# The order of the first MLP block: three columns of h and one of o before any small products, then one run of small products between half columns

## The chip, the cores and the metric

The kernel runs on one core of one Trainium2 chip. The metric is the device time of one launch in microseconds (us); the time of a kernel is the median of its runs. TensorE is called PE below, VectorE DVE, ScalarE ACT, GpSimd POOL, SyncE SP.

## What is computed

Three stages follow each other on float32 data (batch 4, 8 heads, 768 steps, head size 48):

```python
# delta-rule attention: a 48x48 state per batch and head
k_n = k / (np.linalg.norm(k, axis=-1, keepdims=True) + 1e-06)
for t in range(S):
    y[:, :, t] = np.einsum('bhd,bhde->bhe', q[:, :, t], state)
    v_old = np.einsum('bhde,bhd->bhe', state, kt)
    state = state + bt[:, :, :, None] * np.einsum('bhd,bhe->bhde', kt, vt - v_old)
# first MLP, 384 -> 2048 -> 384 on 3072 tokens
h = x @ w_in
g = np.maximum(h, 0.0) + alpha * np.minimum(h, 0.0)
x = g @ w_out
# second MLP, 384 -> 1536 -> 384
g = x @ w_gate
out = (g * (1.0 / (1.0 + np.exp(-g))) * (x @ w_val)) @ w_out
```

## The kernel before

The attention is cut into 24 chunks `c` of 32 steps, and four chunks make a window `w`. Chunk `c` needs, in this order: `do_KS` (product `pk`), `do_QS` (`py`), `do_U` (`pu`, then `U`), `do_S` (the state, products `pst`, then the additions into `St`), `do_Y` (`py`) and `do_XT` (`px`, which gives `xh` and `xl`, the input of the first MLP). All of these products are small: they use 32 or 48 rows of the PE array, and a call of one of these functions is 32 float32 products in the program, which PE runs as 64. `pre_T` (`pt`, four wide transposes) and `pre_G` (`pg`) prepare `q` and `k` of a window, `mask_m` masks one result of `pre_G` on POOL. `lanes` inverts the small triangular matrices of a window on DVE and POOL, step by step; the first one here is that of window 1.

The first MLP takes two chunks of tokens as a block `n` of 256 columns and runs over 16 columns `j` of 128 features. `H1(n, j)` is nine wide products into `h`, ended by one ACT and one DVE instruction that make `pn`. `H1_parts` splits `pn` into a high part (ACT) and a low part (POOL, line 702), both in `gh`. `O1(n, j)` is nine wide products with `gh` into `o`: six with the high part and then three with the low part. `h` and `o` of one `j` are called half columns below. They take their weights from `w1[j]`, which `all_w1` makes from the raw weights pair by pair: DMA, ACT (line 592), three steps on DVE (597, 599, 603), ACT (887) and two subtractions on POOL (875).

The order of all this is written out by hand. Every step is put into a list with a time `u` by `at(u, fn, ...)`, the list is sorted by `u`, and the steps are issued in that order; each engine then runs its instructions strictly in it. The unit of `u` is one column of the first MLP: `H1(n, j)` stands at `16 * n + j`, `O1(n, j)` at 2.5 after it (3.6 for the first column of a later block). The prelude before the list brings chunks 0 and 1 to their end, so that block 0 can start; in the 16 columns of block 0 stand the work on chunks 2 and 3 (which block 1 needs), the rest of `q` of window 1, the remaining conversions of weights, three per column, and from 10.9 on `lanes` of window 1.

Of the kernel before, what the change touches and what calls it, by code (L numbers as in the profile page):

```python
# [24 lines left out]
def kernel(  # L25
# [68 lines left out]
    nat = [ap.tile([128, H, 2, 64], F32, name=f"nat{z}") for z in range(2)]  # L94
# [43 lines left out]
    def half_rows(b):  # L138
        return slice(64 * (b // 2), 64 * (b // 2) + D)
# [19 lines left out]
    def kq_of(c):  # L159
        return kqt[c // 2][:, c % 2]  # L160

    def bank(early, name):
        pool, tag = (ps_h1, "h1") if early else (ps_a, "a")
        return pool.tile([128, 512], F32, name=name, tag=tag)
# [32 lines left out]
    def pre_G(c, parts=(0, 1), early=False, raw=False):  # L197
        w, ci = divmod(c, 4)
        kq = kq_of(c)
        if ci == 0 and 0 in parts:  # L200
            GL[w] = ap.tile([128, 32, C], F32, name="GL", tag="lane" if w > 1 else "TT", bufs=2)
        ps = bank(early, "pg")
        n0, n1 = parts[0], parts[-1] + 1
        for h in range(H):
            for b in BS:
                r = half_rows(b)
                nc.tensor.matmul(  # L207
                    ps[32 * b:32 * b + 32, h * 64 + n0 * C:h * 64 + n1 * C],
                    kq[r, b % 2, h, 0, :],
                    kq[r, b % 2, h, n0:n1, :],  # L210
                    start=True,
                    stop=True,
                    skip_group_check=True,
                )
        gv = ps.rearrange("p (h n i) -> p h n i", h=H, n=2)
        if 0 in parts:
            nc.scalar.activation(out=GL[w][:, ci * 8:ci * 8 + 8, :], in_=gv[:, :, 0, :], func=AF.Copy)
        if 1 in parts:
            mt = ap.tile([128, H, C], F32, name="mt", tag="mt", bufs=6)
            if raw:  # L220
                nc.scalar.activation(out=mt, in_=gv[:, :, 1, :], func=AF.Copy)
            else:
                nc.vector.tensor_tensor(mt, gv[:, :, 1, :], mask.unsqueeze(1).to_broadcast([128, H, C]), ALU.mult)
            m_t[c] = mt
# [88 lines left out]
    def lanes(w, cut):  # L313

        t = Lanes(w)

        def eliminate(i, eng, c0, c1, tmp):

            n, m = C - 1 - i, min(i + 1, c1) - c0
            if m <= 0:  # L320
                return
            w = tmp[:, 0:n * m].rearrange("p (a b) -> p a b", a=n)
            eng.tensor_tensor(  # L323
                w,
                t.L[:, i + 1:C, i:i + 1].to_broadcast([128, n, m]),
                t.X[:, i:i + 1, c0:c0 + m].to_broadcast([128, n, m]),
                ALU.mult,
            )
            yield
            Xv = t.X[:, i + 1:C, c0:c0 + m]  # L330
            eng.tensor_tensor(Xv, Xv, w, ALU.subtract)  # L331

        t.turn(0)
        yield
        t.turn(1)
        GL.pop(w)
        yield
        t.new_X()
        t.norm()
        t.length(0)  # L340
        yield
        for i in range(2):
            r = slice(i * HC, i * HC + HC)
            nc.vector.tensor_tensor(
                t.L[:, :, r], t.L[:, :, r], t.a.unsqueeze(2).to_broadcast([128, C, HC]), ALU.mult
            )
            yield
        size = [max((C - 1 - i) * (min(i + 1, c1) - c0) for i in range(C)) for c0, c1 in ((0, cut), (cut, C))]
        tv = t.new("tmp", "tmp", [128, size[0]])
        tg = t.new("tmg", "tmg", [128, size[1]])  # L350
        for i in range(C - 1):
            todo = [eliminate(i, nc.vector, 0, cut, tv)]
            if i + cut < C - 1:
                todo.append(eliminate(i + cut, nc.gpsimd, cut, C, tg))
            for z in range(2):
                for g in todo:
                    next(g, None)
                t.length(2 * i + z + 1)
            if i == HC:
                TT_t[w] = t.new("TT", "TT", [128, 32, C], 2)  # L360
                t.turn_X(0)
            yield
        t.turn_X(1)
        yield
# [490 lines left out]
    inv0 = []  # L855

    def at(u, fn, *args):
        events.append((u, len(events), fn, args))
# [41 lines left out]
    def go(g, n=1):  # L900
        for _ in range(n):
            next(g, None)
# [101 lines left out]
        return inv  # L1004

    def base(c):
        return {2: 2.9, 3: 7.7, 4: 22.6, 5: 27.2}.get(c, 8 * (c - 2))

    CONV_DONE, CONV_END = 8 + sum(CONVS), 11.0
    CONV_N = 3 * J1 + 1 - CONV_DONE  # L1010
# [2 lines left out]

    for w in range(1, NWIN):
        P = base(4 * w) - 32
        if w == 1:
            for z in range(2):
                at(1.4 + 1.2 * z, lambda: go(inv0[0]))
            for z in range(4):
                at(1.8 + 1.05 * z, pre_T, 1, "q", z // 2, z % 2, nat)  # L1020
            for z in range(4):
                at((5.7, 7.0, 8.8, 10.4)[z], lambda z=z: pre_G(4 + z, raw=True))
                at(13.0 + 2 * z, mask_m, 4 + z)
            for z in range(2):
                at((4.3, 6.4)[z], lambda z=z: pre_G(2 + z, (1,), raw=True))
                at((4.9, 7.5)[z], mask_m, 2 + z)
            l0, l1, n = 10.9, 22.6, LANES
        else:
            if w < TURN:
                at(P - 5, load_nat, w, "k", nat)  # L1030
                for z in range(4):
                    at(P + 1.2 + z, pre_T, w, "k", z // 2, z % 2, nat)
                at(P + 4.5, load_nat, w, "q", nat)
                for z in range(4):
                    at(P + 7.2 + z, pre_T, w, "q", z // 2, z % 2, nat)
            else:
                for z in range(4):
                    at(P - 13 + 1.5 * z, load_split, w, "k", z, nat)
                    at(P - 6.5 + 0.8 * z, turn_T, w, "k", z, nat)
                    at(P - 5.6 + 1.2 * z, load_split, w, "q", z, nat)  # L1040
                    at(P + 3.0 + z, turn_T, w, "q", z, nat)
            at(P - 1, load_beta, w)
            for z in range(4):
                at(P + 11.2 + z, pre_G, 4 * w + z)
            l0, l1, n = P + 15, P + 31.5, LANES
        box = {}

        def step(w=w, box=box):
            if "g" not in box:
                box["g"] = lanes(w, 10)  # L1050
            next(box["g"], None)

        for z in range(n):
            at(l0 + (l1 - l0) * z / n, step)

    at(0.5, do_S, 1)
    at(0.6, load_k2, 2)
    for c in range(2, NCH):
        u = base(c)
        f = {2: 0.8, 3: 0.8, 4: 0.6, 5: 0.6}.get(c, 1.0)  # L1060
        if c > 2:
            at(u - 7, load_v, c)
            at(u - 1.3, load_k2, c)
        at(u - 1.5, scale_v, c)
        at(u + 0.3, do_KS, c)
        at(u + 0.35, do_QS, c)
        at(u + 0.3 + 2 * f, do_U, c)
        at(u + 0.3 + 4 * f, do_S, c)
        at(u + 0.3 + 5 * f, do_Y, c)
        at(u + 0.3 + (7 if c < 4 else 6) * f, do_XT, c)  # L1070
    for n in range(NB1):
        for j in range(J1):
            at(16 * n + j, H1, n, j)
# [33 lines left out]
    for n in range(NB2):  # L1107
        u = E1 + LA + 1 + J2 * n
# [43 lines left out]
```

## Time and profile before

| | us |
|---|---|
| median of 3 runs (1093.03 to 1093.74) | 1093.32 |
| the profiled execution | 1094.43 |
| its span, first to last instruction | 1092.5 |
| PE busy | 1055.2 (97%) |
| DVE busy | 603.6 (55%) |
| ACT busy | 389.9 (36%) |
| POOL busy | 359.5 (33%) |

The profiled execution lies 1.1 us above the median, and 1.9 us of it lie outside its span. In a timeline a row gives the start, the time to the end of its last product, the engine, the line, and in brackets how long the engine stood idle before it and for whom; "issue" is a wait for nothing that the profile shows. The granted clock of PE is 1.0 at 2.4 GHz and 0.5 at 1.2 GHz.

### The profile page before, as it was taken

Reading aid. Unit: us, or ns where it says so; the run is one execution under the profiler, and the core shown is the slowest. Engines: PE = TensorE matmul, PEld = TensorE weight load, DVE = VectorE, ACT = ScalarE, POOL = GpSimd, SP = SyncE. Lnnn points to the kernel's source line nnn. Section 1 sums busy time; section 2 is a strip of 40 time slices with the busy share of each in tenths; the row PEclk is TensorE's granted clock in tenths of the full one; section 3 lists DMA queues with packets and bytes.
Section 4 is the critical chain, followed back from the end, with each engine's and each line's share of the span. In section 5 each row is a group of like instructions: output and inputs, shape, how many; then the busy total and the mean of one; then the engine's idle time right before and its main releaser. Section 6 shows DMA issues by size and latency. Waiting matters only on the chain.

```text
span 1092.5 us, 35673 instructions
## 1 busy us (share of the span) xinstructions
PE 1055.2 (97%) x15649; PEld 969.6 (89%) x15649; DVE 603.6 (55%) x1204; ACT 389.9 (36%) x841; POOL 359.5 (33%) x531
## 2 busy tenths in 40 slices
PE   6689899999999999999999999999999999999998
PEld 5588788999999999999999998888888888888887
DVE  5778865975895697489453453433333333333332
ACT  3556343343434334433444653222222222222211
POOL 3478852832563383366333541101001001010000
PEclk9669999999999999999999999999999999999999
DMA  9663042353344236330441541010010010100001
GB/s 196 184 192 105 10 103 53 62 122 95 70 69 134 66 62 139 90 82 11 118 130 56 159 135 54 1 58 1 1 58 1 18 42 1 58 1 1 29 1 29
DMA packets 165979, 76.34 MB, mean 70 GB/s; under 512 B 129824, under 2 KB 160576, under 8 KB 165824
## 3 DMA queue, kind: packets, MB, share of 16 engines
q1 hardware_dynamic: 160256, 66.28, 24.5%
q10 hardware_dynamic: 5184, 7.37, 2.2%
q8 instruction: 122, 2.00, 0.8%
q0 software_dynamic: 384, 0.41, 0.2%
q14 instruction: 33, 0.27, 0.1%
HBM read 57.52 MB, written 16.52 MB: 68 GB/s over the span
## 4 chain that ended last, share of the span: by engine, by line
PE 89%; POOL 4%; issue 2%; DVE 2%; DMA 1%; ACT 1%; SPq 0%; ACTq 0%; POOLq 0%; DVEq 0%
PE gv L772 27%; PE o L713 18%; PE h L682 18%; PE o L802 14%; PE pst L527 2%; PE pg L207 2%; PE pu L506 2%; PE py L548 2%; PE pk L462 2%; PE py L462 1%; POOL w L875 1%; DMA nat<-in_k_dram 1%; POOL gh L702 1%; POOL X L331 1%; POOL tmg L323 1%
## 5 line engine op out<-in xcount | busy, mean ns | idle before, releaser
L772 PE MATMUL gv<-x2s,w 128*128 128x512 f32 x1296 | 307.6, 391 | 0.0
L772 PEld LDWEIGHTS gv<-x2s,w 128*128 128x128 f32 x1296 | 242.5, 188 | 47.8
L713 PE MATMUL o<-gh,w 128*128 128x256 f32 x1728 | 246.2, 288 | 3.9 <-POOL gh L702 3.9
L682 PE MATMUL h<-xh,w 128*128 128x256 f32 x1152 | 241.2, 286 | 3.0 <-DVE pn L693 1.6
L702 POOL TENSOR_TENSOR gh<-pn,gh 128x256 fp32r<-128x256 f32 x192 | 155.3, 809 | 248.5 <-ACT gh L701 217.3
L713 PEld LDWEIGHTS o<-gh,w 128*128 128x128 f32 x1728 | 217.3, 189 | 11.5 <-POOL gh L702 5.1
L682 PEld LDWEIGHTS h<-xh,w 128*128 128x128 f32 x1152 | 192.2, 191 | 5.8 <-DVE pn L693 2.6
L693 DVE SCALAR_TENSOR_TENSOR pn<-pn,slope,h 128x256 f32<-128x256 f32 x192 | 91.3, 476 | 135.9 <-ACT pn L692 135.9
L682 PE MATMUL h<-xl,w 128*128 128x256 f32 x576 | 163.2, 283 | 0.1
L802 PE MATMUL o<-w,us 128*128 128x384 f32 x864 | 162.5, 337 | 0.0
L802 PEld LDWEIGHTS o<-w,us 128*128 128x128 f32 x864 | 151.9, 188 | 7.1 <-DVE os L815 1.4
L692 ACT ACTIVATE pn<-h,slope 128x256 f32<-128x256 f32 x192 | 90.4, 471 | 137.7 <-PE h L682 134.5
L784 DVE TENSOR_TENSOR sg<-sg,gv 128x512 f32<-128x512 f32 x72 | 49.5, 687 | 151.8 <-ACT sg L782 151.7
L701 ACT ACTIVATE gh<-pn 128x256 fp32r<-128x256 f32 x192 | 80.0, 417 | 145.0 <-DVE pn L693 143.2
L682 PEld LDWEIGHTS h<-xl,w 128*128 128x128 f32 x576 | 109.8, 191 | 0.6 <-DVE xl L574 0.6
L757 POOL TENSOR_TENSOR x2s<-x2r,x2s 128x512 fp32r<-128x512 f32 x15 | 19.3, 1320 | 266.6 <-ACT x2s L755 266.6
L789 ACT ACTIVATE us<-u 128x512 fp32r<-128x512 f32 x72 | 45.5, 632 | 171.2 <-DVE u L785 171.2
L782 ACT ACTIVATE sg<-gv 128x512 f32<-128x512 f32 x72 | 43.0, 597 | 159.3 <-PE gv L772 159.3
L790 DVE TENSOR_TENSOR us<-u,us 128x512 fp32r<-128x512 f32 x72 | 49.9, 693 | 54.8 <-ACT us L789 54.8
L785 DVE TENSOR_TENSOR u<-sg,gv 128x512 f32<-128x512 f32 x72 | 49.5, 688 | 49.3 <-PE gv L772 48.8
L331 DVE TENSOR_TENSOR X<-X,tmp 128x31 f32<-128x31 f32 (+29 forms) x155 | 65.0, 419 | 4.8
L323 DVE TENSOR_TENSOR tmp<-L,X 128x31 f32<-128x31 f32 (+29 forms) x155 | 59.5, 384 | 1.8
(120 smaller groups left out, 975.9 us busy)
## 6 DMA issues: line engine op xcount, KB each, us to landing
w<-in_moe_w_out_dram SPq DMA_DIRECT2D x19, 384.0 KB
wf<-w2d SPq DMA_DIRECT2D x36, 192.0 KB
k<-in_k_dram SPq DMA_DIRECT2D x96, 48.0 KB
x2d<-xs SPq DMA_DIRECT2D x12, 384.0 KB
w<-in_moe_w_gate_dram SPq DMA_DIRECT2D x12, 384.0 KB
w<-in_moe_w_val_dram SPq DMA_DIRECT2D x12, 384.0 KB
x2r<-x2d SPq DMA_DIRECT2D x24, 192.0 KB
v<-in_v_dram SPq DMA_DIRECT2D x88, 48.0 KB
```

Of the source, the lines that this page charges most:

```text
L323: eng.tensor_tensor(w, t.L[:, i + 1:C, i:i + 1].to_broadcast([128, n, m]), t.X[:, i:i + 1, c0:c0 + m].to_broadcast([128, n, m]), ALU.mult,)
L331: eng.tensor_tensor(Xv, Xv, w, ALU.subtract)
L682: nc.tensor.matmul(ps[:, 0:N1], w[:, a, kk * 128:kk * 128 + 128], x[b][:, kk, :], start=(i == 0), stop=(i == 3 * NK - 1),)
L692: nc.scalar.activation(out=g, in_=hv, func=AF.Relu, scale=slope[:, 0, j:j + 1])
L693: nc.vector.scalar_tensor_tensor(out=g, in0=g, scalar=slope[:, 1, j:j + 1], in1=hv, op0=ALU.mult, op1=ALU.add)
L701: nc.scalar.activation(out=gh[:, 0], in_=g, func=AF.Copy)
L702: nc.gpsimd.tensor_tensor(gh[:, 1], g, gh[:, 0], ALU.subtract)
L713: nc.tensor.matmul(o[:, dm // 2, (dm % 2) * N1:(dm % 2) * N1 + N1], w[:, a, dm * 128:dm * 128 + 128], g[:, b], start=(j == 0 and i == 0 an ...
L772: nc.tensor.matmul(p[:, 0:N2], w2[j, z][:, a, kk * 128:kk * 128 + 128], x[:, b, kk], start=(i == 0), stop=(i == 3 * NK - 1),)
L784: nc.vector.tensor_tensor(sg, sg, ps[0], ALU.mult)
L790: nc.vector.tensor_tensor(us[:, 1], u, us[:, 0], ALU.subtract)
L802: nc.tensor.matmul(o2_t[n][t][:, 0:DM], us[:, a, t * 128:t * 128 + 128], w[:, b, :], start=(j == 0 and i == 0), stop=(j == J2 - 1 and i == 2),
```

## The change

Only times in the list change, all of them for the work beside block 0. The first state update (`do_S(1)`) and the load that follows it move from 0.5 to 2.6, so that `H1` of columns 0 to 2 and `O1` of column 0 stand ahead of them. The steps of chunks 2 and 3, the four `pre_T`, the two remaining steps of the prelude's inversion (`go(inv0[0])`), the `pre_G` of window 1 and of chunks 2 and 3, and two of the masks get times that leave one of them, or one with a `pre_T` of four transposes, between any two half columns.

```diff
-        return {2: 2.9, 3: 7.7, 4: 22.6, 5: 27.2}.get(c, 8 * (c - 2))
+        return {2: 3.4, 3: 7.8, 4: 22.6, 5: 27.2}.get(c, 8 * (c - 2))
...
             for z in range(2):
-                at(1.4 + 1.2 * z, lambda: go(inv0[0]))
+                at(3.1 + z, lambda: go(inv0[0]))
             for z in range(4):
-                at(1.8 + 1.05 * z, pre_T, 1, "q", z // 2, z % 2, nat)
+                at((3.7, 4.7, 5.15, 5.65)[z], pre_T, 1, "q", z // 2, z % 2, nat)
             for z in range(4):
-                at((5.7, 7.0, 8.8, 10.4)[z], lambda z=z: pre_G(4 + z, raw=True))
+                at(6.6 + z, lambda z=z: pre_G(4 + z, raw=True))
                 at(13.0 + 2 * z, mask_m, 4 + z)
             for z in range(2):
-                at((4.3, 6.4)[z], lambda z=z: pre_G(2 + z, (1,), raw=True))
-                at((4.9, 7.5)[z], mask_m, 2 + z)
+                at((5.6, 10.6)[z], lambda z=z: pre_G(2 + z, (1,), raw=True))
+                at((6.3, 11.2)[z], mask_m, 2 + z)
...
-    at(0.5, do_S, 1)
-    at(0.6, load_k2, 2)
+    FIRST = {2: (3.6, 4.6, 5.1, 6.1, 7.1, 8.15), 3: (8.1, 9.1, 10.1, 11.1, 12.1, 12.8)}
+    at(2.6, do_S, 1)
+    at(2.7, load_k2, 2)
...
-        f = {2: 0.8, 3: 0.8, 4: 0.6, 5: 0.6}.get(c, 1.0)
+        f = {4: 0.6, 5: 0.6}.get(c, 1.0)
...
+        cols = [u + 0.3 + z * f for z in (0, 0.05, 2, 4, 5, 6)]
+        for x, fn in zip(FIRST.get(c, cols), (do_KS, do_QS, do_U, do_S, do_Y, do_XT)):
+            at(x, fn, c)
```

PE at the start of block 0, before: `h_1025`, `h_1128` and `h_1229` are columns 0, 1 and 2, seven rows each, of which the first stands here.

```order
L682 MATMUL h_1025<-xh,w 128x256
...
L527 MATMUL pst<-U,k_105 64x48 x32
L527 MATMUL pst<-U,k_106 64x48 x32
L682 MATMUL h_1128<-xh,w 128x256
...
L408 MATMUL pi<-TT,GL 32x16 x64
L185 MATMUL pt<-ident,nat_103 128x128 x4
L682 MATMUL h_1229<-xh,w 128x256
...
L713 MATMUL o_1253<-gh,w 128x256 x9
```

Small products stand behind each of the first two columns. PE at the same place, after: columns 0 to 3 are `h_1025`, `h_1056`, `h_1083` and `h_1191`.

```order
L682 MATMUL h_1025<-xh,w 128x256
...
L682 MATMUL h_1056<-xh,w 128x256
...
L682 MATMUL h_1083<-xh,w 128x256
...
L713 MATMUL o_1107<-gh,w 128x256 x9
L527 MATMUL pst<-U,k_105 64x48 x32
L527 MATMUL pst<-U,k_106 64x48 x32
L682 MATMUL h_1191<-xh,w 128x256
...
L408 MATMUL pi<-TT,GL 32x16 x64
L713 MATMUL o_1107<-gh,w 128x256 x9
```

The state update of chunk 1 moved behind columns 0 to 2 of h and column 0 of o. POOL around the mask of chunk 2 (`mt<-mt,mask`), as a difference; `w_120` and `w_121` are the raw weights of columns 10 and 11.

```order
 L702 TENSOR_TENSOR gh<-pn,gh 128x256
-L195 TENSOR_TENSOR mt<-mt,mask 128x256
 L875 TENSOR_TENSOR w<-w_120,w 128x384 x2
 L702 TENSOR_TENSOR gh<-pn,gh 128x256
 L875 TENSOR_TENSOR w<-w_121,w 128x384 x2
+L195 TENSOR_TENSOR mt<-mt,mask 128x256
 L452 TENSOR_TENSOR v<-v,nn 128x384
 L702 TENSOR_TENSOR gh<-pn,gh 128x256
```

The mask moved behind two further conversions. On SP the loads of `v` for chunk 3 now stand ahead of those of `k` for chunk 2. From the first product of column 0 to the state update of chunk 3, PE's stream holds the same products before and after, 1488 of them as PE runs them, and 17 times a half column behind small products where it was 16.

## Rows read from the trace of the kernel before

**Rows 1.** Stretches: length, busy time PE, PEld, DVE, ACT, POOL; clock, DMA, GB/s.
```profile
51.65:68.72 17.07, 14.94 (x326) 13.48 (x326) 12.59 (x19) 8.73 (x16) 8.79 (x9) 0.50 0.75 184
68.72:75.55 6.83, 4.86 (x207) 4.43 (x209) 5.92 (x8) 5.52 (x10) 6.83 (x5) 1.00 0.93 273
75.55:78.96 3.41, 3.41 (x100) 3.29 (x88) 2.81 (x3) 0.00 (x0) 3.41 (x4) 0.50 0.87 276
55.68:112.36 56.68, 52.45 (x1489) 48.00 (x1489) 44.43 (x51) 31.97 (x63) 44.52 (x36) 0.85 0.51 139
112.87:153.30 40.43, 34.90 (x480) 32.19 (x473) 38.17 (x97) 14.34 (x41) 31.33 (x63) 1.00 0.28 56
```

**Rows 2.** The page: busy time of the engines, and PE's instruction queue.
```profile
PE 1055.2 (97%) x15649; PEld 969.6 (89%) x15649; DVE 603.6 (55%) x1204; ACT 389.9 (36%) x841; POOL 359.5 (33%) x531
...
q8 instruction: 122, 2.00, 0.8%
```

**Rows 3.** Timeline of PE, first two columns: start, length, products.
```profile
55.68 0.58 PE L682 MATMUL h<-xh,w 128*128 128x256 f32 x1 [1.37 <-ACT xh L573]
...
58.28 3.67 PE L527 MATMUL pst<-U,k 32*64 32x48 f32 x128
61.88 0.58 PE L682 MATMUL h<-xh,w 128*128 128x256 f32 x1
...
64.09 1.90 PE L408 MATMUL pi<-TT,GL 32*32 32x16 f32 x128
```

**Rows 4.** Timeline of PE, the waits for "issue" and the runs around them.
```profile
69.90 1.26 PE L430 MATMUL pi<-tmp,Dm 16*32 16x16 f32 x128
...
72.74 0.61 PE L462 MATMUL pk<-St,kqt 48*32 48x48 f32 x35
75.32 0.62 PE L462 MATMUL pk<-St,kqt 48*32 48x48 f32 x27 [1.97 <-issue]
...
80.76 0.78 PE L207 MATMUL pg<-kqt 48*32 48x32 f32 x64
...
84.28 0.49 PE L185 MATMUL pt<-ident,nat 128*128 128x128 f32 x3 [0.41 <-issue]
...
89.10 0.99 PE L207 MATMUL pg<-kqt 48*32 48x32 f32 x64
...
94.12 0.76 PE L207 MATMUL pg<-kqt 48*32 48x64 f32 x40 [1.21 <-issue]
...
98.14 1.10 PE L462 MATMUL pk<-St,kqt 48*32 48x48 f32 x64
...
101.85 0.27 PE L462 MATMUL py<-St,kqt 48*32 48x48 f32 x3 [0.56 <-issue]
...
112.36 1.15 PE L527 MATMUL pst<-U,k 32*64 32x48 f32 x64
```

**Rows 5.** The chain that ended last, in order of time: start, length, what.
```profile
71.75 1.06 PE h L682 x9
...
81.54 1.25 PE o L713 x9
```

**Rows 6.** Timeline of POOL: conversions, low part of gh, mask.
```profile
60.53 2.17 POOL L875 TENSOR_TENSOR w<-w,w 128x384 fp32r<-128x384 f32 x2 [2.49 <-ACT w L887]
62.65 1.45 POOL L702 TENSOR_TENSOR gh<-pn,gh 128x256 fp32r<-128x256 f32 x1
...
86.63 0.74 POOL L195 TENSOR_TENSOR mt<-mt,mask 128x256 f32<-128x256 f32 x1
...
92.34 2.71 POOL L875 TENSOR_TENSOR w<-w,w 128x384 fp32r<-128x384 f32 x2
```

**Rows 7.** Timeline of ACT: a conversion of weights.
```profile
90.60 0.92 ACT L887 ACTIVATE w<-w 128x768 fp32r<-128x768 f32 x1
```

**Rows 8.** Timeline of DVE where the lanes of window 1 begin.
```profile
114.28 1.02 DVE L538 TENSOR_TENSOR St<-pst,St 128x384 f32<-128x384 f32 x2
115.22 1.08 DVE L269 STREAM_TRANSPOSE L<-GL 128x512 f32<-128x512 f32 x1
```

More of the change, by code (lines that the diff above doesn't have):

```diff
@@ L1064 @@
         at(u - 1.5, scale_v, c)
[L1065 to L1070, printed above, removed]
+        cols = [u + 0.3 + z * f for z in (0, 0.05, 2, 4, 5, 6)]
+        for x, fn in zip(FIRST.get(c, cols), (do_KS, do_QS, do_U, do_S, do_Y, do_XT)):
+            at(x, fn, c)
     for n in range(NB1):
```

## The prediction

> **What bounds the kernel now.** I read the stretches first, for the clock and for the engine that is full; then PE's timeline from the first column on, for what it waits for; then POOL and DVE where PE's work meets theirs.
>
> Between the first product of column 0 (55.68) and the state update of chunk 3 (112.36), PE is busy for 52.45 of 56.68 us [rows 1, 3, 4]. No other engine is as full, so this stretch is PE's. Two things make it longer than its products. The granted clock is half (1.2 GHz) up to 68.72 and again from 75.55 to 78.96, and full (2.4 GHz) between and afterwards [rows 1]. And PE stands idle four times, 1.97, 0.41, 1.21 and 0.56 us, in all 4.15, each time in the middle of a run of equal products and for nothing that the profile shows [rows 4].
>
> These four waits have a common place. PE has 15649 products and as many weight loads, and its instruction queue moved 122 packets [rows 2]: 31298 / 122 = 256 instructions, that is 128 products to a packet. Counting products in the timeline from one wait to the next gives 253, 255 and 256, two packets each. So I read the waits as PE arriving at the end of a packet before the next one is there. From the edge before to the end of the wait it took: 70.3 (48th product of the run at 69.90) to 75.32, 5.0 us; 80.9 (the run at 80.76) to 84.28, 3.4; 89.6 (the run at 89.10) to 94.12, 4.5; 98.2 (the run at 98.14) to 101.85, 3.6 [rows 4]. The mean is 4.1 us to a packet, the ends are 3.4 and 5.0. A packet whose products take longer shows no wait.
>
> After 112.36 the stretch belongs to DVE: 38.17 busy of 40.43 us from 112.87 to 153.30, where the lanes of window 1 run [rows 1]. Their second transposition (115.22) stands behind the two additions into the state at 114.28, and these wait for the state update of chunk 3 [rows 8]. Columns of h wait for DVE there; and after that stretch PE is full again to the end. So what moves the start of this chain moves the end of the kernel by as much, and I make the sum up to it.
>
> **The change part by part.** From the first product of column 0 to the state update of chunk 3 the products are the same, 1488, and their number makes the packets end at the same counts. What differs is the clock at which they run, how they fall into packets, and the waits.
>
> *The clock.* Before, half clock beyond column 0 lasts from 58.28 to 68.72 and from 75.55 to 78.96, 13.85 us. At full clock the same kinds take: pst 2 x 1.15 for 3.67 [rows 3, 4], pi 1.26 for 1.90 [rows 3, 4], a column of h 1.25 for 2.21 (61.88 to 64.09) [rows 3, 5]: six tenths. So the half clock costs 13.85 x 0.4 = 5.5 us. After, PE runs 27 wide products of h from 55.68 without a gap. Before, the clock rose while wide products stood together (column 2 and o of column 0 at 68.7) and fell after PE had stood still for 1.97 us. I take the rise at the end of column 2. Columns 1 and 2 then run at half clock, 1.95 each (2.21 less 0.2 that a column behind small products takes longer), 2 x (1.95 - 1.06) = 1.8 us more than at full [rows 3, 5]. Bounds: a rise at the end of column 0 costs nothing of that, one at 68.7 as before costs up to 2 us more. Gain taken: 5.5 - 1.8 = 3.7.
>
> *o of column 0.* Columns 1 and 2 end at 58.28 + 2 x 1.95 = 62.2, six products with the high part at 62.9. The low part is on POOL behind a conversion, from 62.65 to 64.10 [rows 6], and up to there POOL's order is the same. PE waits 1.2 us; queued behind it are the state update of chunk 1 and everything else on PE. Before, this o came at 68.7 and waited for nothing. Bounds: 0.5, if the clock is still half, to 1.4.
>
> *The packets.* After, PE reaches the first edge (53 products into pst) at 64.5 + 0.9 = 65.4. Prices at full clock: 1.25 for a half column behind small products [rows 5], 1.1 for 64 of pst, 0.8 for a narrow and 1.05 for a wide run of 64, 1.2 for 128 of pi [rows 4], 0.44 for four transposes (0.49 for three and the pipeline's end [rows 4]). The eleven packets up to the state update of chunk 3 hold 3.0, 2.5, 2.9, 4.1, 3.1, 4.7, 4.1, 3.0, 4.4, 4.1 and 3.9 us of products. The first, for one, is 75 of pst, column 3 of h and 44 of pi: 1.3 + 1.25 + 0.4. Where this is under 4.1, PE waits for the rest: 1.1 + 1.6 + 1.2 + 1.0 + 1.1 + 0.2 = 6.2 us. Before it was 4.15, so the loss is 2.1: small products at full clock use up a packet in less than it takes to bring one, where at half clock they hid it (58.28 to 68.72 shows no wait at all). With 3.4 us to a packet the waits are 2.5, a gain of 1.7; with 5.0 for all they would be 15, and with 5.0 for the first five alone, where DMA is as busy as before 78.96 (0.75 to 0.93 against 0.51 over the whole stretch [rows 1]), 10.7.
>
> The Trainium skill (Runtime: NRT & Kernel Launch, "Instruction fetch mechanics") says that instructions come in blocks of 256, fetched while the block before runs, and that crossing a boundary is mostly hidden. The trace agrees with the 256 and not with the hiding, 1.97 us at one edge [rows 2, 4]. By the page alone the waits would be none, and the sum 6.2 us lower.
>
> *The mask of chunk 2.* It stood on POOL at 86.63, 9.4 us before its reader, the py of `do_Y(2)` [rows 6]. Now it stands behind the conversion for column 11. By the packets above, column 6 of h ends at 87.9; ACT then has its activation (0.5) and two conversions of 0.9 [rows 7], POOL 2.71 for the conversion and 0.74 for the mask [rows 6]: 93.6. PE comes to `do_Y(2)` at 92.5 (pst, o, pg, h). It waits 1.1 us, and o of column 5 and all behind it with it. Bounds: 0, if PE is later or POOL's two subtractions take 2.17 as at 60.53, to 1.5.
>
> *The rest.* One more half column behind small products costs 0.2 (1.25 against 1.06 [rows 5]). The loads on SP, the conversions on ACT and DVE, and the transposes' copies keep their number and lie beside PE; if PE were faster, DVE, with 44.43 of 56.68 us [rows 1], would be next.
>
> *The lanes' start.* Before, the state update began at 112.36 and took 1.15, but its additions began only at 114.28 [rows 4, 8], because the first transposition of the lanes stood ahead of them on DVE and waited for ACT's copy of its last `pg`, which stood behind the last conversion of weights. Now that copy stands ahead of this conversion and of column 10's activation, and the additions can follow the state update at once (113.5 in the times of before): 0.8 us gained. Bounds: 0 and 0.9.
>
> Sum: -3.7 + 1.2 + 2.1 + 1.1 + 0.2 - 0.8 = +0.1 us. The sum is made against the profiled execution (1094.43, span 1092.5), which lies 1.1 above the median; what differs lies inside the span, so I carry it to the median: 1093.32 + 0.1 = 1093.4. **Forecast: no change that can be measured.** The measurement of this kernel can tell about 0.2%, 2.2 us, from none.
>
> **The rivals.** *The stream keeps up (faster).* Each run of small products now has a half column on both sides, and if a packet comes in 3.4 us as at 84.28, the waits are 2.5: 0.1 - 3.7 = -3.6, so 1089.7. Against it: in three of four waits it took longer, and in the stretch in question DMA is busiest. Chance 0.16. *The stream is hidden altogether*, as the page has it: no waits, 0.1 - 6.2 = -6.1, 1087.2. Four waits in the trace speak against it. Chance 0.04.
>
> *The stream falls behind (slower).* With the full clock at 62 us, five packets of 2.5 to 4.1 us of products stand one behind the other, while the weights are still being loaded. If each takes 5.0 us, as the one at 75.32 did, the waits are 10.7, 4.5 more than taken: +4.6, 1097.9. It decides from about 4.5 us to a packet, where the loss passes 2.2. For it: the two longest of the four lie where DMA is busy. Against: in the new order fewer loads may be under way. Chance 0.24.
>
> *The clock does not rise before 68.7*, so that the change does not do what it says: columns 1 and 2, o and pst at half clock, up to 2 us more, of which the packets hide about one, since pst at half clock outlasts a packet. +1.1, 1094.4, still no change. Chance 0.08.
>
> **How the numbers follow.** Forecast 0.48 and the late clock 0.08 make 0.56 for a time within 0.2%; the two faster cases 0.20; the slower one 0.24. The range goes from 3.6 us to a packet (waits of 3.5, 2.7 less: 1090.7) to 4.7 for the first five (waits of 9.2, 3.0 more: 1096.4); what lies beyond, somewhat under half of the outer cases, is under 0.2. The likeliest's own range is 1091.2 to 1095.6.
>
> **What would show it.** Right: full clock at about 62 us and no fall after it; a wait of o for POOL's gh of 0.5 to 1.4 us near 63; waits for "issue" of 5 to 7 us between 64 and 112, at least three of them before 86; a wait of py for POOL's mask near 93; the state update of chunk 3 within 2 us of 112.4, with its additions at once behind it. Wrong: "issue" under 3 us or over 9; a second fall of the clock; a conversion or DVE, and not PE, that ends the wait for a column in this stretch; a start of the lanes' chain that does not move the end.

## The result, and the profile after

The changed kernel takes 1099.68 us (median of 8 runs, 1097.45 to 1101.72) where the kernel before takes 1093.53 in the same comparison (8 runs, 1092.07 to 1096.12). The ratio over all these runs is 1.0051, with a 95% interval of 1.0035 to 1.0068: slower by half a percent, 5.6 us by that ratio (6.2 between the two medians). The forecast was no change, and its range ended at 1096.4. The profiled execution lies at 1099.33, its span at 1097.4, 4.9 us over the span before.

The page of the changed kernel shows that the work is the same: PE has as many products, and its instruction queue as many packets, as in [rows 2].

```profile
PE 1053.6 (96%) x15649; PEld 968.2 (88%) x15649; DVE 605.1 (55%) x1204; ACT 390.3 (36%) x841; POOL 358.4 (33%) x531
...
q8 instruction: 122, 2.00, 0.8%
```

The first thing to see lies ahead of the point where the sum of the prediction began. Column 0 of h starts at 59.03, not at 55.68 [rows 3]. Followed backwards in the changed kernel's timelines of PE, ACT and SP (start, length, what; in brackets the idle time before it and what ended it), each is late by the one ahead of it: h by the copy xh of `do_XT(1)`, this by px, px by ACT's copy ys, and ys, which had stood idle for 5.09 us, by "DMA v".

```profile
59.03 0.58 PE L682 MATMUL h<-xh,w 128*128 128x256 f32 x1 [1.03 <-ACT xh L573]
...
57.10 0.90 PE L570 MATMUL px<-ident,ys 128*128 128x128 f32 x3 [2.83 <-ACT ys L557]
...
56.09 0.36 ACTq L608 DMA_DIRECT2D w<-in_moe_w_out_dram  x1
56.55 0.49 ACT L557 ACTIVATE ys<-py 128x384 f32<-128x384 f32 x1 [5.09 <-DMA v<-in_v_dram]
...
50.02 7.23 SPq L123 DMA_DIRECT2D v<-in_v_dram  x8
69.54 5.64 SPq L123 DMA_DIRECT2D k<-in_k_dram  x8
```

The copy ys does not read v. Ahead of it in ACT's queue stands the issue of a load, w_out of column 7, and that is what waits. In the kernel before the same two instructions stood at 52.37 and 52.86, with 2.29 us of waiting for PE and none for a load:

```profile
52.37 0.38 ACTq L608 DMA_DIRECT2D w<-in_moe_w_out_dram  x1
52.86 0.49 ACT L557 ACTIVATE ys<-py 128x384 f32<-128x384 f32 x1 [2.29 <-PE py L548]
...
50.98 2.37 SPq L123 DMA_DIRECT2D v<-in_v_dram  x4
60.25 1.80 SPq L123 DMA_DIRECT2D k<-in_k_dram  x4
```

On SP, eight loads of v now go out in a row where there were four; the four of chunk 3 had stood behind those of k for chunk 2. As the program is built, the loads of SP and ACT share eight counters in turn, and a load is issued only when the earlier load on its counter has landed. Before, w_out of column 7 followed a load of q on its counter (q landed at 52.34, w_out was issued at 52.37). Now three of the four moved loads are dealt a counter ahead of it, so it comes three counters later in the turn, behind the first load of v for chunk 2, which lands at 56.07; it is issued at 56.09. The Trainium skill (DMA: Bandwidth & Descriptors, "Anatomy of one DMA — SWDGE (gpsimd) path") says that DMA engines wait on no semaphore, and that any such wait is on the engine that issues. The trace agrees: the 5.09 us are on ACT.

The second thing is the stretch from column 0 to the state update of chunk 3. It took 56.68 us before [rows 1] and takes 59.67 now. The view of stretches (length; busy time of PE, PEld, DVE, ACT, POOL; clock, DMA share, GB/s) shows a clock that rises early and falls twice more:

```profile
59.03:62.74 3.71, 3.70 (x15) 3.40 (x16) 3.63 (x5) 1.00 (x2) 2.36 (x2) 0.50 0.68 219
62.74:69.56 6.82, 4.16 (x103) 3.76 (x104) 6.68 (x7) 5.06 (x9) 5.66 (x5) 1.00 0.63 194
69.56:72.98 3.42, 3.42 (x73) 3.33 (x64) 3.38 (x5) 1.59 (x3) 3.42 (x3) 0.50 0.65 178
72.98:100.28 27.30, 20.82 (x770) 18.58 (x773) 20.81 (x26) 14.57 (x30) 19.70 (x17) 1.00 0.64 179
100.28:103.70 3.42, 3.42 (x74) 3.08 (x65) 2.81 (x2) 2.47 (x4) 2.44 (x3) 0.50 0.02 5
59.03:118.70 59.67, 50.52 (x1488) 45.72 (x1489) 47.71 (x52) 33.65 (x66) 44.90 (x37) 0.91 0.45 129
```

Half clock is 10.5 us of it, against 16.45 before, and PE is busy for 1.9 us less. What grew is PE's waiting, 9.1 us against 4.15 [rows 4]. Its rows in the timeline of PE, and then, for the two waits on POOL, POOL's rows that end them:

```profile
64.19 0.98 PE L713 MATMUL o<-gh,w 128*128 128x256 f32 x6
67.83 0.62 PE L713 MATMUL o<-gh,w 128*128 128x256 f32 x3 [2.66 <-POOL gh L702]
...
77.34 0.54 PE L462 MATMUL pk<-St,kqt 48*32 48x48 f32 x30 [1.13 <-issue]
...
80.89 0.55 PE L430 MATMUL pi<-tmp,Dm 16*32 16x16 f32 x43 [0.53 <-issue]
...
85.72 0.38 PE L682 MATMUL h<-xh,w 128*128 128x256 f32 x1 [0.67 <-issue]
...
91.25 0.33 PE L207 MATMUL pg<-kqt 48*32 48x32 f32 x16 [2.14 <-issue]
...
99.85 1.17 PE L548 MATMUL py<-U,mt 32*32 32x48 f32 x64 [2.01 <-POOL mt L195]
100.94 2.29 PE L713 MATMUL o<-gh,w 128*128 128x256 f32 x9
...
118.70 1.15 PE L527 MATMUL pst<-U,k 32*64 32x48 f32 x64
```

```profile
63.90 2.87 POOL L875 TENSOR_TENSOR w<-w,w 128x384 fp32r<-128x384 f32 x2 [2.51 <-ACT w L887]
66.74 1.03 POOL L702 TENSOR_TENSOR gh<-pn,gh 128x256 fp32r<-128x256 f32 x1
...
95.46 2.93 POOL L875 TENSOR_TENSOR w<-w,w 128x384 fp32r<-128x384 f32 x2 [2.82 <-ACT w L887]
98.36 1.44 POOL L195 TENSOR_TENSOR mt<-mt,mask 128x256 f32<-128x256 f32 x1
```

The waits for "issue" are as long as before, 4.5 us in all. New are 2.66 us for POOL's gh and 2.01 us for POOL's mask, and behind each the clock falls (69.56 and 100.28); the o at 100.94 then takes 2.29 where it takes 1.3.

The third is the start of the lanes on DVE. The additions into the state stand at once behind the state update, and the second transposition comes 2.12 us after its start (2.86 before [rows 4, 8]).

```profile
119.88 1.02 DVE L538 TENSOR_TENSOR St<-pst,St 128x384 f32<-128x384 f32 x2
120.82 1.13 DVE L269 STREAM_TRANSPOSE L<-GL 128x512 f32<-128x512 f32 x1
```

So the profile adds up to 3.35 (column 0 late) + 2.99 (the stretch) - 0.74 (the lanes) = 5.60 at that transposition, and 4.9 at the end.

### The profile page after: what moved, and what is told of

It reads as the page before. It is cut to its first block, busy times and chain, and to the rows that moved or that the text cites. A ratio compares the mean times of both kernels' runs of the same rounds, so it can differ in the third digit from the quotient of the medians.

```text
span 1097.4 us, 35673 instructions
## 1 busy us (share of the span) xinstructions
PE 1053.6 (96%) x15649; PEld 968.2 (88%) x15649; DVE 605.1 (55%) x1204; ACT 390.3 (36%) x841; POOL 358.4 (33%) x531
## 4 chain that ended last, share of the span: by engine, by line
PE 89%; POOL 4%; issue 3%; DMA 2%; SPq 1%; ACT 0%; DVE 0%; ACTq 0%; POOLq 0%; DVEq 0%
PE gv L772 27%; PE o L713 19%; PE h L682 18%; PE o L802 14%; PE pst L527 2%; PE pg L207 2%; PE pk L462 2%; PE pu L506 2%; PE py L548 2%; PE py L462 1%; POOL w L875 1%; SPq L105 1%; POOL tmg L323 1%; POOL X L331 1%; POOL gh L702 1%
```

## The experiments

Each was compared with the kernel before on its own chip; ratios to that are what is compared, and 0.1% is 1.1 us. A reading of all fourteen profiles comes behind the single runs.

**The loads of v behind those of k again (e1_v3_late).**

```diff
-            at(u - 7, load_v, c)
+            at(2.75 if c == 3 else u - 7, load_v, c)
```

> The changed kernel with one call moved: the four loads of v for chunk 3 are listed behind those of k for chunk 2 again (due time 2.75), as they stood before the change. Theory A (a load's counter): the loads share eight counters in turn, and a load waits until the earlier load on its counter has landed. In the changed kernel the w_out load of column 7 on ScalarE's queue shares one with the first load of v for chunk 2 (landed 56.07), was issued at 56.09 and held ScalarE's copy ys behind it (wait 5.09 us), so that column 0 of h began at 59.03 instead of 55.68. Here it shares one with a load of q (landed near 52.3): issue near 52.4, no wait of ys on v, column 0 near 55.7, and the time about 3.3 us under the changed kernel's (1096.3 where that is 1099.7). Theory B (eight loads at once crowd each other and the loads behind them): column 0 near 55.7 too, but the v loads of chunk 2 land earlier than 56. Theory C (the late start has another cause, such as the clock, or is made up by a later wait): column 0 near 59, or the time within 1 us of the changed kernel's.

Ratio 1.0045 (1.0030 to 1.0060). The timelines of ACT and PE show the cause of the late start as theory A had it: w_out goes out at 51.60, ended by a load of q, and column 0 starts at 55.33.

```profile
51.60 0.40 ACTq L608 DMA_DIRECT2D w<-in_moe_w_out_dram  x1
52.10 0.49 ACT L557 ACTIVATE ys<-py 128x384 f32<-128x384 f32 x1 [1.90 <-DMA nat<-in_q_dram]
...
55.33 0.58 PE L682 MATMUL h<-xh,w 128*128 128x256 f32 x1 [1.78 <-ACT xh L573]
```

But the time fell by 0.7 us only, not by 3.3, which is what theory C had for the time. In this profile 20.3 us between column 0 and the state additions of chunk 3 are at half clock, 10.5 in the changed kernel's. Whether that is the rule stayed open here (see the chain below).

**The other way round: the kernel before, with v ahead of k (e2_v3_early).**

```diff
-            at(u - 7, load_v, c)
+            at(0.45 if c == 3 else u - 7, load_v, c)
```

> The kernel before with one call moved: the four loads of v for chunk 3 are listed ahead of the state update of chunk 1 (due time 0.45), so that they stand ahead of those of k for chunk 2 as in the changed kernel; nothing else of the change is made. Theory A (a load's counter): the w_out load of column 7 shares its counter with the first load of v for chunk 2, is issued near 56.0 instead of 52.37, the copy ys waits about 5 us on v, column 0 of h begins near 59.0 instead of 55.68, and the time is about 3.3 us above the kernel before (1096.8 where that is 1093.5). Theory C (the late start is another part's doing, or a later wait makes it up): column 0 near 55.7, or the time within 1 us of the kernel before.

Ratio 1.0028 (1.0015 to 1.0040): +3.1 us for four loads issued earlier, as theory A said, with the same signs on ACT and PE:

```profile
57.66 0.38 ACTq L608 DMA_DIRECT2D w<-in_moe_w_out_dram  x1
58.15 0.49 ACT L557 ACTIVATE ys<-py 128x384 f32<-128x384 f32 x1 [5.07 <-DMA v<-in_v_dram]
...
60.63 0.58 PE L682 MATMUL h<-xh,w 128*128 128x256 f32 x1 [1.04 <-ACT xh L573]
```

**Counter or traffic: half of the loads (e6_v3_half).**

```diff
-        load_steps(t, v, c, eng)
+        load_steps(t, v, c, eng, 0, 2 if c == 3 else 4)
...
             at(u - 7, load_v, c)
+            if c == 3:
+                at(2.75, lambda: load_steps(v_t[3], v, 3, nc.sync, 2, 4))
```

> The changed kernel with half of the moved loads put back: two of the four loads of v for chunk 3 stay ahead of those of k for chunk 2, two are listed behind them (due time 2.75). Theory A (a load's counter): the w_out load of column 7 now shares its counter with the last load of q, which landed at 55.90 in the changed kernel, so it is issued near 55.9 instead of 56.09, and nothing is won: column 0 of h begins near 58.9, the time is within 0.6 us of the changed kernel's. Theory B (the number of loads ahead, or the traffic that they make): half of the delay is won, column 0 begins near 57.4, and the time is 1.7 us under the changed kernel's.

Ratio 1.0058 (1.0045 to 1.0070), the changed kernel's, and column 0 starts at 58.91. With two of the four loads gone nothing is won, since w_out now follows on the counter of the last q load, which lands as late. It is the counter, not the number of loads or their traffic:

```profile
55.96 0.37 ACTq L608 DMA_DIRECT2D w<-in_moe_w_out_dram  x1
56.43 0.49 ACT L557 ACTIVATE ys<-py 128x384 f32<-128x384 f32 x1 [5.21 <-DMA nat<-in_q_dram]
```

**The mask of chunk 2 ahead of a conversion (e3_mask_early).**

```diff
-                at((6.3, 11.2)[z], mask_m, 2 + z)
+                at((5.9, 11.2)[z], mask_m, 2 + z)
```

> The changed kernel with one call moved: the masking of chunk 2's products on GpSimd is listed at 5.9 instead of 6.3, ahead of the conversion of w_out for column 11. Theory A: the wait of PE for the mask (py <- mt, 2.01 us near 99.85) goes to under 0.3 us, the clock does not fall at 100.3, the product o that took 2.29 us at half clock takes 1.26, and the conversion of w_out moves about 1.4 us later without anyone waiting for it; the start of column 0 stays near 59. The time is 2 to 3.5 us under the changed kernel's (1096.2 to 1097.7 where that is 1099.7). Rival: the product o of the same column, or the sum gh on GpSimd, is late by what the mask came earlier (a wait o <- gh of 1.5 us or more behind 96), and the time stays within 0.7 us of the changed kernel's.

Ratio 1.0042 (1.0027 to 1.0057), 1.0 us under the changed kernel: less than theory A had it, and well inside the intervals. The wait is gone and so is the fall of the clock behind it. In this profile the timeline of PE has another fall instead, 6.8 us at half clock from 78.47, behind a wait for "issue" that was 1.13 us in the changed kernel:

```profile
66.77 0.62 PE L713 MATMUL o<-gh,w 128*128 128x256 f32 x3 [2.67 <-POOL gh L702]
...
77.02 0.54 PE L462 MATMUL pk<-St,kqt 48*32 48x48 f32 x30 [1.87 <-issue]
```

**Both edits (e4_both).** The diffs are those of the first and the fourth experiment.

> The edits of e1_v3_late and e3_mask_early together: v of chunk 3 listed behind k of chunk 2, and the mask of chunk 2 ahead of the conversion of w_out for column 11. The stretch from column 0 of h to the state update of chunk 3 is read as a sum: work of PE at full clock, about 0.4 us for each us of half clock, and PE's waits; what lies behind it took 977.4 to 978.2 us in all six profiles so far. Theory A (the sum holds): column 0 starts near 55.5, the wait for the mask is gone, the wait of o for gh of 2.7 us near 61 to 64 stays, and the time is 2 to 2.5 us under e1_v3_late (1096.5 to 1097 where that is 1099.0). Rival (the clock takes it back: what is won in waits comes back as a longer stretch at half clock): no wait for the mask, but over 18 us at half clock between column 0 and the state update, and the time within 0.8 us of e1_v3_late.

Ratio 1.0016 (1.0002 to 1.0030): 3.2 us under the first experiment, 3.8 under the changed kernel. The sum held, and the gain was over the 2 to 2.5 expected: this profile has only 8.5 us at half clock; the wait for gh (2.18 us, at 65.33) stays.

**And the state update of chunk 1 ahead of o of column 0 (e5_both_s1).**

```diff
-    at(2.6, do_S, 1)
-    at(2.7, load_k2, 2)
+    at(2.3, do_S, 1)
+    at(2.4, load_k2, 2)
```

> e4_both, and the state update of chunk 1 (with the loads of k behind it) listed ahead of the product o of column 0 (2.3 and 2.4 instead of 2.6 and 2.7), so that its 128 products lie over the GpSimd work that makes gh. Theory A: the wait o <- gh of 2.7 us shrinks to under 0.7 us, the other waits stay as in e4_both, and the time is 2 to 3 us under e4_both, near the kernel before (1093.5 to 1095). Rival 1 (the small products need their instructions fetched, and GpSimd is not late by a fixed time): the wait goes over to issue, over 6.5 us of issue waits between column 0 and the state update of chunk 3, and the time stays within 0.8 us of e4_both. Rival 2 (the packets are worth something once their waits are gone): 1092 or less.

Ratio 0.9990 (0.9980 to 1.0000), 2.8 us under the kernel without this edit. o waits 0.49 us for gh; the longest wait left is 2.46 us for "issue". One wait that theory A did not have came in, 1.24 us of `pi` for DVE's pn.

**The state update of chunk 1 back in column 0 (e7_s1_back)**, the rest of the change kept; then the mask earlier as well (e8_s1_mask).

```diff
-    at(2.6, do_S, 1)
-    at(2.7, load_k2, 2)
+    at(0.5, do_S, 1)
+    at(0.6, load_k2, 2)
```

> The changed kernel with one part of the change undone: the state update of chunk 1 and the loads of k for chunk 2 stand at 0.5 and 0.6 again, behind column 0 of h, as before the change; the packets behind column 2 and the order of the rest stay as changed. Loads of v for chunk 3 then stand behind those of k by themselves. Theory A (the change loses by what it put ahead, not by the packets): column 0 begins near 55.7, the wait of o for gh is under 0.7 us, that for the mask (2.0) stays, and the time is 3.5 to 5 us under the changed kernel's (1094.7 to 1096.2). Rival (the packets lose, by their instruction waits): issue waits over 6 us between column 0 and the state update of chunk 3, and the time over 1097.

> e7_s1_back, and the mask of chunk 2 listed ahead of the conversion of w_out for column 11 as in e3_mask_early. What stays of the change is the packets and their order. Theory A: no wait of PE for GpSimd over 0.7 us between column 0 and the state update of chunk 3, and a time 2 to 2.5 us under e7_s1_back, equal to the kernel before within 1 us (1092.5 to 1094.5): the packets neither win nor lose. Rival 1 (packets win): under 1092.5. Rival 2 (packets lose): over 1095, with issue waits over 6 us or over 18 us at half clock.

Ratios 1.0024 (1.0012 to 1.0035) and 1.0022 (1.0012 to 1.0032). The first came 3.0 us under the changed kernel, half a microsecond less than expected. The second should have won 2 us more and won nothing: Rival 2 had its time, but not by its signs. The wait for the mask is gone, but the issue waits rose from 2.8 to 4.0, and both kernels wait 2.2 and 1.6 us for DVE's pn of column 2 ahead of `pi`; in e8_s1_mask:

```profile
70.62 1.26 PE L408 MATMUL pi<-TT,GL 32*32 32x16 f32 x128 [1.64 <-DVE pn L693]
```

What e8_s1_mask has of the change is the packets and their order, and it is 2.4 us over the kernel before, clear of noise: put in alone, they lose. The half clock is not what they lose by, 17.1 us against 16.5, nor are the issue waits, 4.0 against 4.2. The wait for pn is new, and column 0 starts 0.8 us later in this profile; together that is 2.4 us, and the state additions come 2.1 later.

In both kernels the clock rises at 65.8 and 66.7, 10 us after column 0 starts. In e5_both_s1, where the state update stands ahead of o instead, it rises 3.9 us after. The stretch from column 0 to the state additions, for e8_s1_mask and then for the same edits with the state update ahead of o (their second execution, below):

```profile
56.45:116.39 59.94, 54.27 (x1553) 49.56 (x1553) 47.28 (x53) 34.27 (x67) 45.91 (x38) 0.86 0.48 132
```

```profile
56.84:113.01 56.17, 50.95 (x1553) 46.18 (x1553) 47.72 (x54) 33.80 (x67) 47.52 (x38) 0.92 0.50 140
```

**The chain, once more on one chip.** What was open was the first experiment's shortfall.

> The changed kernel once more, as the first step of a chain of four on one chip, in which each kernel takes away one cost that the next does not have. What is open: e1_v3_late won 3.7 us at the start of column 0 but only 0.7 us of the median. In the profiles so far 15 of 20 waits of PE of 1.8 us or more between column 0 and the state update of chunk 3 stood at a fall of the granted clock to 0.5 (within 2.1 us of the wait's end), and no fall stood elsewhere; a fall gave 3.4 to 10.2 us at half, at about 0.4 us lost for each. Theory A (each wait costs itself and, three times in four, a fall): three or four waits of 1.8 us or more, falls at two or three of them, column 0 near 59, time near 1099.5 (0.5% over the kernel before). Theory C (e1_v3_late's shortfall is the rule): the same time, see the next.

> The kernel of e1_v3_late once more (v of chunk 3 behind k of chunk 2). Theory A: column 0 near 55.5, the waits of 1.8 us or more are those of the changed kernel (gh, one of issue, mask), and the number of falls at them is two or three by chance, so that the second profile need not show 20.3 us at half again; the median is 2.5 to 3.5 us under f1_after. Theory C (an earlier column 0 makes the clock worse): over 16 us at half between column 0 and the state update again, and the median within 1 us of f1_after.

> The kernel of e4_both once more (and the mask of chunk 2 ahead of the conversion). Theory A: the wait for the mask is gone, 2.0 us and a fall worth 1.4 in most runs, less what the instruction fetch takes back (issue waits stay at 4 to 5 us in all): 2 to 3.4 us under f2_v3. Rival: the issue wait grows by what the mask wait was, within 1 us of f2_v3.

> The kernel of e5_both_s1 once more (and the state update of chunk 1 ahead of the product o of column 0). Theory A: the wait for gh is under 0.7 us instead of 2.2 to 2.7, one wait of 1.8 us or more is left instead of two; 2 to 3.5 us under f3_v3_mask, and 0.5 to 1.5 us under the kernel before, since only half clock is left to differ. Rival: equal to the kernel before within 0.5 us, the packets worth nothing.

| kernel | ratio, first | ratio, again (95%) | mean, us over before |
|---|---|---|---|
| changed | 1.0051 | 1.0055 (1.0040 to 1.0071) | +5.8 |
| v behind k | 1.0045 | 1.0036 (1.0022 to 1.0051) | +4.4 |
| and mask earlier | 1.0016 | 1.0025 (1.0016 to 1.0034) | +2.2 |
| and state update ahead of o | 0.9990 | 0.9992 (0.9982 to 1.0002) | -1.0 |

By the means the three edits win 1.4, 2.2 and 3.2 us, in all 6.8. The last and the whole are clear of the intervals in both series. The other two hang on the company: the loads' order was worth 0.7 and 2.1 us next to the changed kernel, 2.8 where the mask was early already (e3_mask_early against e4_both), and 3.1 alone; the mask's place 3.2 and 1.2 in the chain, but 1.0 alone and 0.2 in e8_s1_mask. In the second series that step missed its forecast and came out nearly as its rival had it: 1.2 us by the ratio, with issue waits of 6.6 us where the kernel ahead of it has 2.8. So the wait for the mask is seen in the profiles, but that it costs more than the issue waits take back is not shown.

The second execution of the kernel with v behind k shows how the loads' cost can be smaller than in the kernel before. w_out goes out early, at 52.59, and yet column 0 starts at 57.95: the products ahead of it ran at half clock from 34.3 on, so PE itself is late, and ys waits for PE and not for a load. In such an execution a load that lands at 56 costs only what PE does not lose anyway; how often that is so is not known.

```profile
52.59 0.36 ACTq L608 DMA_DIRECT2D w<-in_moe_w_out_dram  x1
55.44 0.49 ACT L557 ACTIVATE ys<-py 128x384 f32<-128x384 f32 x1 [2.63 <-PE py L548]
...
57.95 0.58 PE L682 MATMUL h<-xh,w 128*128 128x256 f32 x1 [1.06 <-ACT xh L573]
```

It had 17.4 us at half clock, so theory C's sign came true, but its time did not: the median is 2.2 us under the changed kernel's, and that kernel had 16.9 this time. With two profiles of each (10.5 and 16.9, 20.3 and 17.4), whether an earlier column 0 costs clock stays open. In the last of the chain PE's timeline shows the cover that the change had taken away, the state update between the columns and their o, with no wait for gh:

```profile
62.76 2.08 PE L527 MATMUL pst<-U,k 32*64 32x48 f32 x128
64.77 1.52 PE L713 MATMUL o<-gh,w 128*128 128x256 f32 x9
```

**All profiles together.** From column 0 to the state additions of chunk 3 (DVE, L538), with the time at half clock and PE's waits inside it:

| profile | column 0 | additions | half clock | waits: issue, other |
|---|---|---|---|---|
| before | 55.68 | 114.28 | 16.5 | 4.2, 0 |
| changed | 59.03 | 119.88 | 10.5 | 4.5, 4.7 |
| changed, again | 58.88 | 118.98 | 16.9 | 2.8, 3.3 |
| v behind k | 55.33 | 119.24 | 20.3 | 3.5, 4.7 |
| v behind k, again | 57.95 | 119.40 | 17.4 | 2.8, 4.7 |
| before, v ahead | 60.63 | 118.15 | 11.2 | 5.5, 0 |
| half of v | 58.91 | 119.58 | 19.0 | 2.2, 3.9 |
| mask | 57.98 | 117.18 | 13.7 | 3.2, 2.7 |
| v and mask | 56.53 | 113.77 | 8.5 | 4.1, 2.2 |
| v and mask, again | 56.95 | 115.58 | 4.3 | 6.6, 2.5 |
| v, mask, state update | 57.86 | 115.29 | 10.7 | 4.0, 1.7 |
| the same, again | 56.84 | 113.01 | 8.7 | 3.9, 1.2 |
| state update in column 0 | 56.11 | 115.97 | 16.5 | 2.8, 4.2 |
| and mask | 56.45 | 116.39 | 17.1 | 4.0, 1.6 |

Three things can be read from it. The stretch is 48.0 us + 0.36 for each us of half clock + the waits, to within 0.5 us in thirteen of fourteen (1.1 in one). What lies behind the additions to the end of the span is 977.4 to 978.2 us in all fourteen, wherever they stand: a shift there moves the end one to one. And the clock: with three columns of h ahead it rises 3.2 to 5.3 us after column 0 starts (ten profiles); with the 128 products of the state update behind column 0, after 4.4, 9.7, 10.3 and 13.0 us.

## Why the prediction was wrong, point by point

**The step that failed** is the one with which the sum began. It started at the first product of column 0 and took its time of before, without giving a reason, and it said that the loads on SP "keep their number and lie beside PE". The part on the change had shown that the loads of v for chunk 3 now stand ahead of those of k for chunk 2; nothing was asked of what else such a load decides. It cost 3.35 us in the profile, 3.1 us when made alone in the kernel before, and 1.4 us by the mean of the chain. At 1.4 us alone the time would have stayed in the range; with o of column 0, which was mis-sized, it left it.

**o of column 0** was mis-sized: 1.2 us taken, 0.5 to 1.4 as bounds, 2.66 measured, and 2.1 to 2.7 in every kernel with that order. Two errors add up. The six products with the high part ended 6.1 us after column 0 began, not 7.2, because the clock rose within column 1; and POOL ended its gh 8.7 us after it, not 8.4, its two subtractions taking 2.87 us where [rows 6] had 2.17, and the gh 0.4 less. That is no chance of one run: the pair took 2.86 to 2.91 in the ten profiles with three columns of h ahead and 2.16 to 2.17 in the four others. The faster PE came earlier to an engine that had not become faster. And behind the wait the clock fell again, which the sum did not have. By the chain this term is the largest: taking the wait away won 3.2 us.

**The mask** was mis-sized: 1.1 us taken, 0 to 1.5 as bounds, 2.01 measured. PE came to `do_Y(2)` 4.6 us after the end of column 6, as worked out. POOL was late: 2.93 + 1.44 us for conversion and mask, where [rows 6] gave 2.71 + 0.74. Half of the mask's time was missing. It took 1.44 us in all six kernels in which it stands behind that conversion and 0.73 to 0.75 in the six in which it stands ahead of it, so a row of the old place was no price for the new one; why it is longer there is not shown. What the term cost in time is not shown either (see the chain).

**The clock** was right in kind and too large. The rise at 62.74 meets the sign in the text ("about 62") by luck: the text had it 6.5 us behind the start of column 0, at the end of column 2, and it came 3.7 behind a start that was 3.35 late. The gain was 5.9 us less at half clock, 2.1 us at 0.36, where 3.7 was taken; "no fall after it" was wrong. That columns of h ahead bring the full clock early, and that this is worth time, fits e8_s1_mask against e5_both_s1 and its second execution: 6.4 to 8.5 us more at half clock, 2.3 to 3.1 us at 0.36, where the mean ratio differs by 3.4. It is not certain in a single run: with v ahead in the kernel before, the clock rose 4.4 us after column 0 in spite of the state update there.

**The packets** were over-priced: 6.2 us of issue waits expected, 4.5 measured, 2.2 to 6.6 with a mean of 3.7 in the twelve profiles of kernels with the new order. The new waits seem to have paid for a part of these: the mean is 3.1 in the six profiles with over 3 us of other waits and 4.3 in the six with less. That the instruction stream goes on meanwhile would explain it, and is argued, not shown. The rival of a stream that falls behind had the right sign and almost the size, 1097.9, for a reason that the trace refutes: no stretch shows 10.7 us, and behind the edges the longest wait is 2.46 us.

**The lanes' start** was right: 0.74 us gained, 0.8 taken, additions at once behind the state update. That their start moves the end one to one was right as well.

With the measured terms the sum is 3.35 + 4.99 (waits) - 2.1 - 0.74 = +5.5 us at the lanes' start, where the profile shows 5.60. The prediction's chance of 0.24 for slower was placed on the wrong mechanism; the costs that came true were a reordered load, which it left out, and two waits for POOL, which it had and made too small.

## What to carry to other kernels

When a change moves a load, ask not only which engines issue it and read it, but which later load inherits its place in the shared counters, and what stands behind that load in its engine's queue. When it makes one engine faster or takes a piece of work from between a producer and its reader, price the wait with the slowest row of the other engine, not with the one that happens to stand in the trace, and add what the clock loses behind it. And part a list of edits: here the order of the columns won 3.4 us over the same packets with the state update in column 0, once that update was put between them and their o, where it hides the wait; the packets alone lost 2.4. That version is 0.1% under the kernel before in both comparisons (0.9980 to 1.0000 and 0.9982 to 1.0002), at the edge of what can be measured.

## What had not been expected of the hardware

An idle PE can cost twice here. In the fourteen profiles there are 29 waits of PE of 1.8 us or more between column 0 and the state additions. Behind 20 of them, at most 2.1 us after the wait's end, or in the wait itself, the granted clock fell from full to half, and it fell nowhere else in that stretch. A fall gave 3.4 to 10.2 us at half, and at 0.36 that is 1.2 to 3.7 us on top of the wait. Nine such waits had no fall, three of them in one execution, so a single profile cannot tell what a kernel usually loses by it. Runs of one kernel lie up to 8 us apart, and the mean granted clock of each run tells a part of that: within a kernel the slower runs have the lower clock, with a correlation of -0.45 over the 123 runs of the changed kernels, a fifth of the variance. How much of the remaining 1.0 us under the kernel before is the clock's, and how much the packets', stays open.
